# Key gradients transposed by DMA in pairs, in the upper attention layer's backward pass of a four-layer kernel on one Trainium2 core

## The chip, the core and the metric

The kernel runs on one core of one Trainium2 chip. The metric is the time of one execution on the device in microseconds, as the median of several runs. A profile is one further execution, taken with the hardware profiler on. The engines are TensorE (PE for its matmuls, PEld for its weight loads, which run beside matmuls), VectorE (DVE), ScalarE (ACT), GpSimd (POOL) and SyncE (SP), which issues the DMAs; the profile calls the queue of an issuing engine SPq. Data in SBUF lies on 128 partitions; matmul results go to PSUM, which has eight banks.

## The reference

Four residual layers alternate: linear attention (A), gated linear unit (B), A, B, on 2048 tokens of width 512, with weights shared by the two A and by the two B. The kernel returns the output and all gradients for a given output gradient.

```python
def _A_ref(x, wqkv, wo):                      # H = 32 heads of 16
    q, k, v = ...                             # x @ wqkv, split in heads
    phi = lambda t: jnp.where(t > 0, t + 1, jnp.exp(t)) + 1e-6
    pq, pk = phi(q), phi(k)
    kv = jnp.einsum("bhsd,bhse->bhde", pk, v)
    z = jnp.einsum("bhsd->bhd", pk)
    num = jnp.einsum("bhqd,bhde->bhqe", pq, kv)
    den = jnp.einsum("bhqd,bhd->bhq", pq, z)[..., None] + 1e-6
    ...                                       # num / den, heads joined, @ wo
def _B_ref(x, w_gate, w_up, w_down):
    ...                                       # (sigmoid(x @ w_gate) * (x @ w_up)) @ w_down
x = x + _A_ref(_layernorm(x), A_wqkv, A_wo)
x = x + _B_ref(_layernorm(x), B_w_gate, B_w_up, B_w_down)
x = x + _A_ref(_layernorm(x), A_wqkv, A_wo)
x = x + _B_ref(_layernorm(x), B_w_gate, B_w_up, B_w_down)
```

## The kernel before

The tokens are worked on in 16 tiles of 128; two tiles are a pair (`NB2 = 2`). The kernel goes forward through layers 0 to 3, saving what the backward pass needs to DRAM (`sv`), and then backward: `b_bwd_p1` for layer 3, `a_bwd_p1` for layer 2 (the upper attention layer), `b_bwd_p1` for layer 1, `a_bwd_p1` for layer 0, and a tail. The change touches `a_bwd_p1` alone.

Weight gradients are sums over all tokens, so they are made apart, by the object `W` of class `P2`. Its jobs (`b_jobs`, `a_jobs`) each have a "set": one operand of all 16 tiles, up to 1 MB, loaded by one DMA into one of three buffers (`p2_set`, L1363). A job is cut into units, `W.run(n)` runs n of them wherever the code calls it. A unit of the jobs in question is 16 matmuls (L1511); a job has four, its result is evacuated by ScalarE (L1487) in two halves and stored (L1468). When a job's first unit is run, the loads up to two jobs on are called (`prefetch`).

`a_bwd_p1` has two halves. The first makes the query gradients dq and stores them to DRAM. The second (from L1661) is the one of the change. Before its loop, pairs 0 and 1 are loaded (L1702): pk, the key features; dq; hT, the transposed layer input; h, the layer input. A small chain of products follows with units between. Then comes a loop over the 16 tiles (L1772). For tile `st`:

- tiles 0 to 3 transpose dq and pk on TensorE into PSUM (L1785, tile `T2_ps`) and copy them with ScalarE to `pdT`; later tiles find them transposed by the load (L1692, L1674);
- four matmuls give the gradient of the key features (`dpk_ps`, L1791), VectorE multiplies it by the derivative (`dphk`, L1794, and `dk`, L1796, into the pair's tile `dkst`), and on odd tiles the pair is stored (`dqk_store`, L1535);
- on even tiles the next pair's loads are called (`load`, L1802), on odd ones h (L1806);
- VectorE adds the tile before the last to the residual gradient (`add`, L1088 and L1089), and POOL casts it (L292);
- `finish` of the previous tile: twelve matmuls into one bank `dh_ps` (L1756), four each with dqT, pkT and dkT as weights, then the layer norm's backward sums (L1076 on ScalarE, L1081 on VectorE);
- four transposes of this tile's dk on TensorE (L374, `t_ps<-ident,dkstage`) and a copy to `dkT` on ScalarE (L383).

Units are run before the loop, in tile 0 (where there is nothing to finish) and behind the loop; then `W.run(W.left() - HOLD)` (L319) runs all but six of what is left before layer 1 begins. The order of the four computing engines is that of the code. The order of SP's DMAs is not: the framework's scheduler places each DMA in SP's queue when, in its own plan of the run, what it depends on is done and a buffer of its tile's name is free; of those ready, the earlier in the code goes first, and `tc.issue_after` ties one behind another. Tiles of one name in pool `stg` (pk_ld, dq_ld, pkT, hT_ld, h_ld, dkstage) have two buffers.

Of the kernel before, what the change touches and what calls it, by code (L numbers as in the profile page):

```python
# [9 lines left out]
BF16 = mybir.dt.bfloat16  # L10
# [12 lines left out]
P = 128  # L23
NST = S // P
NDC = D // P
# [5 lines left out]
NB = 4  # L31
# [337 lines left out]
def transpose_blocks(k, ps_pool, dst, src_blocks, evac, tag="tp"):  # L369
    nc = k.nc  # L370
    n = len(src_blocks)
    ps = ps_pool.tile([P, 8, P], BF16, name=tag, tag=tag)
    for i, sb in enumerate(src_blocks):
        nc.tensor.transpose(ps[:, i, :], sb, k.ident[:])  # L374
    evac_copy(k, dst, ps[:, 0:n, :], evac)
# [454 lines left out]
def attn_fronts(k, A, pool, small):  # L830
# [38 lines left out]
    def front3(st, bank="ln", evac="scalar"):  # L869
        if st >= NST:  # L870
# [4 lines left out]
                         evac, tag="ln_tp" if bank == "ln" else f"{bank}_ps")  # L875
        f["T"] = pqnT

    def attn_mm(st):
        if st >= NST:
            return  # L880
        pqnT = F_[st]["T"]
        y_ps = F_[st]["y"] = ps_tile(k, "y", [P, D], F32, "y_ps")
# [20 lines left out]
def ab_fwd(k, A, ln, side, nxt=None, out_cb=None, last_cb=None):  # L903
# [3 lines left out]
    with ExitStack() as ctx:  # L907
# [6 lines left out]

        def gu(T, hT, fs, later=False):
            c0, w = FSL[fs]
            ssd_t, hh_t = T["ssd"], T["hh"]
            g_ps = ps_tile(k, "g", [P, 512], F32, "g_ps")
# [15 lines left out]

        def transposes(T, fs):
            hh_t, hhT = T["hh"], T["hhT"]
            fcs = fchunks_of_slice(fs)
# [132 lines left out]
class LnBwd:  # L1070
# [15 lines left out]
    def add(self):  # L1086
        nc = self.k.nc
        nc.vector.scalar_tensor_tensor(self.t[:], self.h, self.ab[:, 1:2], self.t[:], ALU.mult, ALU.add)  # L1088
        nc.vector.scalar_tensor_tensor(self.x[:], self.t[:], self.ab[:, 0:1],  # L1089
                                       self.x[:] if self.res is None else self.res, ALU.add, ALU.add)  # L1090
# [308 lines left out]
class P2:  # L1399
# [7 lines left out]
    def load(self, l, nm, pool=None, part=None):  # L1407
        k, R = self.k, self.R
        src = k.sv[l]["h" if nm == "h" else "gbf"]
        if (l, nm) not in self.ops:  # L1410
            self.ops[l, nm] = (pool or R.big).tile([P, NST, D], BF16, name="p2_a1" if nm == "h" else "p2_a2")
            self.todo[l, nm] = list(range(NST // NB))
        t, todo = self.ops[l, nm], self.todo[l, nm]
        for b in ([part] if part is not None else list(todo)):
            todo.remove(b)
            R.eng().dma_start(out=t[:, b * NB:(b + 1) * NB, :], in_=dram_batch(src, b))
# [115 lines left out]
def dqk_store(k, sv, half, b, src):  # L1532
    n = D // GW
    for g in range(n):
        ins = k.nc.sync.dma_start(out=sv["dqk"][half * n + g, b], in_=src[:, :, g * GW:(g + 1) * GW])  # L1535
    return ins.ins


def a_bwd_p1(k, R, l, W, mk_out_cb=None):
    nc, tc = k.nc, k.tc  # L1540
    sv = k.sv[l]
# [3 lines left out]
    NB2 = 2  # L1545
    with ExitStack() as ctx:
# [9 lines left out]
        with tc.tile_pool(name=f"ab_stg1{l}", bufs=3, side="right", reuse_waits="tile") as stg, \  # L1556
# [60 lines left out]
            for st in range(NST):  # L1617
                with tc.issue_after(k.mt_load):
                    ph_st = phld.get(st)
                T = dict(st=st, ph=ph_st, ph_pair=phld.cur)  # L1620
# [18 lines left out]
                if st >= 1:  # L1639
                    dq_ops(Ts[st - 1])  # L1640
                if st >= DZLAG:
                    accum_dz(Ts[st - DZLAG])
                Ts.append(T)
# [17 lines left out]
        with tc.tile_pool(name=f"ab_stg2{l}", bufs=2, side="right", reuse_waits="tile") as stg, \  # L1661
                tc.tile_pool(name=f"ab_work2{l}", bufs=2, side="right", reuse_waits="tile") as work, \
                tc.tile_pool(name=f"ab_late{l}", bufs=1, reuse_waits="tile") as late:
            pkld = BatchLoader(k, stg, sv["pk"], "pk_ld", nb=NB2)
            hTld = BatchLoader(k, stg, sv["hT"], "hT_ld", nb=NB2)
            hld = BatchLoader(k, stg, sv["h"], "h_ld", nb=NB2)
            out_cb = mk_out_cb(stg) if mk_out_cb is not None else None
            LD, LDH = {}, {}
            pkT = {}
# [7 lines left out]
            def load(p):  # L1677
                if p >= NST // NB2:
                    return
                st0 = p * NB2  # L1680
                pkld.get(st0)
                dq = stg.tile([P, NB2, D], BF16, name="dq_ld")
                if st0 < NB:
                    for g in range(D // GW):
                        nc.sync.dma_start(out=dq[:, :, g * GW:(g + 1) * GW], in_=sv["dqk"][g, p])
                hTld.get(st0)
                if st0 >= NB:
                    dq = dq[:].rearrange("p n d -> p (n d)").rearrange("p (c t) -> p c t", c=NDC)
                    with tc.issue_after(hTld.ins.ins):
                        n = GW // P  # L1690
                        for g in range(D // GW):
                            nc.sync.dma_start(out=dq[:, g * n:(g + 1) * n, :],  # L1692
                                              in_=sv["dqk"][g, p].rearrange("p n w -> (p n) w"), transpose=True)
                        load_pkT(p)
                LD[p] = dict(pk=pkld.cur, dq=dq, hT=hTld.cur)

            def load_h(p):
                if p < NST // NB2:
                    hld.get(p * NB2)
                    LDH[p] = hld.cur  # L1700

            for p in range(2):  # L1702
                load(p)
                load_h(p)
            Nv = late.tile([P, NDC, D], BF16, name="Nv")
            Mv = late.tile([P, NDC, D], BF16, name="Mv")
# [42 lines left out]
            def finish(T):  # L1749
                st = T["st"]  # L1750
                dh_ps = ps_tile(k, "y", [P, D], F32, "dh_ps")
                ops = [(T["dqT"][:, c, :], k.wqkvT[:, c, :]) for c in range(NDC)]
                ops += [(T["pkT"][:, c, :], Mv[:, c, :]) for c in range(NDC)]
                ops += [(T["dkT"][:, c, :], k.wqkvT[:, NDC + c, :]) for c in range(NDC)]
                for i, (lhsT, rhs) in enumerate(ops):
                    nc.tensor.matmul(dh_ps[:], lhsT=lhsT, rhs=rhs, start=(i == 0), stop=(i == len(ops) - 1))  # L1756
                T["ln"] = LnBwd(k, work, small, dh_ps[:], T["h"], k.rstd[l][:, st:st + 1], k.xs[st])
                T["ln"].sums()

            def add(T):  # L1760
                T["ln"].add()
                if out_cb is not None:
                    out_cb(T["st"])
# [3 lines left out]
                nc.scalar.copy(ps[:], dzb[:])  # L1767
                return ps

            prev = prev2 = None  # L1770
            dpk_ps = dpk_begin()
            for st in range(NST):  # L1772
                L = LD[st // NB2]
                e = st % NB2
                pk_st, hT_st = L["pk"][:, e, :], L["hT"][:, e, :]
                T = dict(st=st, h=LDH[st // NB2][:, e, :])
                if e == 0:
                    dkst = stg.tile([P, NB2, D], BF16, name="dkstage")
                own = st < NB
                if own:  # L1780
                    pdT = work.tile([P, 2, NDC, P], BF16, name="pdT")
                    tps = ps_tile(k, "t", [P, 2, NDC, P], BF16, "T2_ps")
                    for a, src in enumerate((L["dq"][:, e, :], pk_st)):
                        for c in range(NDC):
                            nc.tensor.transpose(tps[:, a, c, :], src[:, c * P:(c + 1) * P], k.ident[:])  # L1785
                    nc.scalar.copy(pdT[:], tps[:])
                    T["dqT"], T["pkT"] = pdT[:, 0, :, :], pdT[:, 1, :, :]
                else:
                    T["dqT"], T["pkT"] = L["dq"][:, :, e:NB2 * P:NB2], pkT[st // NB2][:, :, e * P:(e + 1) * P]
                for c in range(NDC):  # L1790
                    nc.tensor.matmul(dpk_ps[:], lhsT=hT_st[:, c * P:(c + 1) * P], rhs=Nv[:, c, :],  # L1791
                                     start=False, stop=(c == NDC - 1), skip_group_check=True)
                dphk = work.tile([P, D], BF16, name="dphk")
                nc.vector.tensor_scalar(dphk[:], pk_st, -EPS, 1.0, ALU.add, ALU.min)  # L1794
                dk = dkst[:, e, :]
                nc.vector.tensor_tensor(dk, dpk_ps[:], dphk[:], ALU.mult)  # L1796
                if e == NB2 - 1:
                    dqk_store(k, sv, 1, st // NB2, dkst[:])
                if st + 1 < NST:
                    dpk_ps = dpk_begin()  # L1800
                if e == 0 and st > 0:
                    load(st // NB2 + 1)  # L1802
                if prev2 is not None:
                    add(prev2)
                    if e == 1:
                        load_h(st // NB2 + 1)  # L1806
                if prev is not None:
                    finish(prev)
                    next(smalls, None)
                else:  # L1810
                    W.run(1)
                dkT = work.tile([P, NDC, P], BF16, name="dkT")
                transpose_blocks(k, k.ps["t"], dkT[:], [dk[:, c * P:(c + 1) * P] for c in range(NDC)], "scalar",
                                 tag="t_ps")
                T["dkT"] = dkT
                prev, prev2 = T, prev
            drain(smalls)
            add(prev2)
            W.run(1)
            finish(prev)  # L1820
            add(prev)


DZLAG = 4
GTLOAD = {4: 2, 6: 3}
SMALL = (("kvbd", P), ("dkvbd", P))
WIDE = ("G", "X")
# [78 lines left out]
```

## Time and profile before

| | us |
|---|---|
| median of 3 runs (1133.23 to 1135.18) | 1133.44 |
| the profiled execution | 1135.02 |
| its span, first to last instruction | 1133.3 |
| TensorE busy in the span | 1109.4 |
| VectorE, ScalarE, POOL busy | 706.9, 484.2, 291.2 |
| loop of the upper layer's second half | 603.1 to 667.2 |
| units alone behind it | 667.2 to about 730 |

The profile is read by lines and tiles of the program: `L1756` is a line of the kernel, `dh_ps<-Mv,pkT` what an instruction writes and reads. A timeline row gives start, duration, engine, line and form; back-to-back matmuls overlap in their durations, so their cost is the distance of their starts. The table by stretches gives busy time of each engine (with the number of instructions), the granted clock of TensorE, the share of the DMA engines and their rate. A DMA has two times: that of its issue on SP, and its landing, when its semaphore is complete.

### The profile page before, as it was taken

To read this page: it belongs to the slowest core of one execution; us is meant where nothing else is said; L and a number is where in the kernel's file an instruction comes from. 1 tells how busy PE (TensorE), PEld (TensorE's weight loads), DVE (VectorE), ACT (ScalarE), POOL (GpSimd) and SP (SyncE) were. 2 spreads that over 40 slices of the span, in tenths; PEclk is the share of its full clock that TensorE was granted. 3 is DMA by queue.
4 is the path that set the end of the run, shared out by engine and by line. 5 is a ranking of instruction groups with operands and counts; after the bars stand their busy time and mean duration, and the time that the engine had idled before them with its cause. 6 is when DMAs were issued, how large, how long until landed. Compare 5 with 4: busy or idle time off the path is not lost.

```text
span 1133.3 us, 20011 instructions
## 1 busy us (share of the span) xinstructions
PE 1109.4 (98%) x7468; PEld 648.8 (57%) x7468; DVE 706.9 (62%) x1344; ACT 484.2 (43%) x909; POOL 291.2 (26%) x518
## 2 busy tenths in 40 slices
PE   8979999998999999999999999999999999999998
PEld 4444554444555555554456468855546745448888
DVE  6788886778776456664975850166664976852211
ACT  6676666555756543433625431224324515410000
POOL 5647776435666400000110220000000110210000
PEclk9999999999999999999999999999999999999999
DMA  8967999855899999997899997799998899969996
GB/s 270 309 197 212 273 282 283 245 142 183 223 294 265 269 261 262 302 255 207 222 244 313 220 260 237 195 283 289 257 283 260 205 282 289 241 194 298 263 205 192
DMA packets 413682, 282.36 MB, mean 249 GB/s; under 512 B 198608, under 2 KB 399504, under 8 KB 409744
## 3 DMA queue, kind: packets, MB, share of 16 engines
q1 hardware_dynamic: 412432, 280.03, 90.3%
q8 instruction: 58, 0.95, 0.3%
q10 hardware_dynamic: 1152, 1.05, 0.3%
q14 instruction: 40, 0.33, 0.1%
HBM read 125.44 MB, written 115.70 MB: 213 GB/s over the span
## 4 chain that ended last, share of the span: by engine, by line
PE 89%; DVE 6%; DMA 3%; ACT 1%; issue 1%; POOL 0%; DVEq 0%; SPq 0%; POOLq 0%
PE p_ps L1511 18%; PE dh_ps L1252 13%; PE dh_ps L1756 7%; PE p_ps L1495 7%; PE y_ps L956 6%; PE dhh_ps L1110 6%; PE g_ps L922 6%; PE u_ps L922 6%; PE T_ps L1209 3%; PE dpk_ps L1791 2%; PE GT_ps L1652 2%; PE dp_ps L1624 2%; PE y_ps L884 2%; PE t_mm L616 2%; PE X_ps L624 2%; PE t_ps L374 1%
## 5 line engine op out<-in xcount | busy, mean ns | idle before, releaser
L1511 PE MATMUL p_ps<-p_set,p_a 128*128 128x256 bf16 (+1 forms) x2032 | 210.1, 264 | 0.0
L1511 PEld LDWEIGHTS <-p_a 128*128 128x128 bf16 x2048 | 185.9, 98 | 22.2
L1132 DVE TENSOR_TENSOR dd<-dhh_ps,ssd 128x512 bf16<-128x512 f32 x144 | 82.4, 629 | 121.3 <-PE dhh_ps L1110 117.4
L930 POOL TENSOR_TENSOR ssd_t<-hh_t,oms 128x512 bf16<-128x512 bf16 (+1 forms) x96 | 100.7, 1060 | 50.1 <-ACT out_t L226 13.5
L1252 PEld LDWEIGHTS <-ddT 128*128 128x128 bf16 (+1 forms) x704 | 67.6, 98 | 74.6 <-DMA ddT<-dd 2.4
L922 PEld LDWEIGHTS <-hT 128*128 128x128 bf16 x768 | 72.5, 98 | 65.2 <-DVE hT L381 1.4
L1084 POOL TENSOR_SCALAR ab<-c 128x2 f32<-128x2 f32 x64 | 12.4, 194 | 377.9 <-DVE junk L1081 364.7
L1211 ACT COPY ddT<-T_ps 128x1024 bf16<-128x1024 bf16 (+1 forms) x72 | 58.8, 819 | 115.2 <-PE T_ps L1209 62.0
L1076 ACT ACTIVATE t_sb<-dh_ps,rstd_all 128x512 f32<-128x512 f32 x64 | 44.0, 688 | 115.7 <-issue 65.0
L922 PE MATMUL g_ps<-wg,hT 128*128 128x512 bf16 (+1 forms) x384 | 90.0, 357 | 0.4 <-DVE hT L381 0.4
L924 ACT ACTIVATE ssd_t<-g_ps 128x512 bf16<-128x512 f32 (+1 forms) x96 | 53.4, 556 | 86.1 <-PE g_ps L922 80.3
L922 PE MATMUL u_ps<-wu,hT 128*128 128x512 bf16 (+1 forms) x384 | 90.0, 357 | 0.0
L1485 DVE TENSOR_TENSOR dw_stg<-p_ps,dw_stg 128x512 bf16<-128x512 f32 (+3 forms) x43 | 28.1, 653 | 98.1 <-PE p_ps L1511 81.4
L929 DVE TENSOR_TENSOR hh_t<-u_ps,ssd_t 128x512 bf16<-128x512 f32 (+1 forms) x96 | 60.4, 631 | 44.0 <-PE u_ps L922 34.2
L1252 PE MATMUL dh_ps<-wgT,ddT 128*128 128x512 bf16 (+1 forms) x352 | 85.2, 379 | 0.0
L1252 PE MATMUL dh_ps<-wuT,ddT 128*128 128x512 bf16 (+1 forms) x352 | 81.3, 379 | 0.8 <-DMA ddT<-dd 0.7
L956 PE MATMUL y_ps<-wd,hhT 128*128 128x512 bf16 (+1 forms) x352 | 81.3, 379 | 0.6 <-DVE x L958 0.6
L1495 PE MATMUL p_ps<-p_a,p_set 128*128 128x512 bf16 (+1 forms) x352 | 81.2, 379 | 0.0
L1110 PE MATMUL dhh_ps<-wdT,gTb 128*128 128x512 bf16 x336 | 74.2, 357 | 0.0
L956 PEld LDWEIGHTS <-hhT 128*128 128x128 bf16 (+1 forms) x352 | 34.2, 98 | 41.1 <-issue 0.7
L1081 DVE SCALAR_TENSOR_TENSOR junk<-t_sb,h_ld 128x512 bf16<-128x512 f32 x48 | 37.2, 774 | 28.9 <-ACT t_sb L1076 23.7
L926 ACT ACTIVATE oms<-g_ps 128x512 bf16<-128x512 f32 (+1 forms) x96 | 52.8, 550 | 3.9 <-POOL ssd_t L930 3.7
(227 smaller groups left out, 1824.2 us busy)
## 6 DMA issues: line engine op xcount, KB each, us to landing
p_set<-sv_hdd SPq DMA_DIRECT2D x30, 1024.0 KB, 6.2
sv_ssd<-ssd_t SPq DMA_DIRECT2D x32, 688.0 KB, 4.2
ssd<-sv_ssd SPq DMA_DIRECT2D x24, 688.0 KB, 5.1
sv_hdd<-dd SPq DMA_DIRECT2D x24, 512.0 KB, 5.0
sv_hdd<-hh_t SPq DMA_DIRECT2D x32, 320.0 KB, 4.4
p_a<-sv_h SPq DMA_DIRECT2D x16, 512.0 KB, 6.5
p_set<-sv_dqk SPq DMA_DIRECT2D x8, 1024.0 KB, 7.5
h_ld<-sv_h SPq DMA_DIRECT2D x24, 256.0 KB, 4.7
```

Source lines behind the costliest of these rows:

```text
L922: nc.tensor.matmul(ps[:, 0:w], lhsT=hT[:, kc, :], rhs=w_sb[:, kc, c0:c0 + w], start=(kc == 0), stop=(kc == NDC - 1))
L924: nc.scalar.activation(ssd_t[:, 0, c0:c0 + w], g_ps[:, 0:w], ACT.Sigmoid)
L929: nc.vector.tensor_tensor(hh_t[:, c0:c0 + w], u_ps[:, 0:w], ssd_t[:, 0, c0:c0 + w], ALU.mult)
L930: nc.gpsimd.tensor_tensor(ssd_t[:, 1, c0:c0 + w], hh_t[:, c0:c0 + w], oms[:, 0:w], ALU.mult)
L956: nc.tensor.matmul(y_ps[:], lhsT=T["hhT"][0:r, fc, :], rhs=k.wd[0:r, fc, :], start=(fc == 0), stop=(fc == NFC - 1))
L1110: k.nc.tensor.matmul(ps[:, 0:w], lhsT=gT[:, jc, :], rhs=k.wdT[:, jc, c0:c0 + w], start=(jc == 0), stop=(jc == NDC - 1))
L1132: k.nc.vector.tensor_tensor(dd_part(dd, a, fs), ps[:, 0:w], ssd[:, a, c0:c0 + w], ALU.mult)
L1211: nc.scalar.copy(out[:, :, 0:nfull, :], tps[:, :, 0:nfull, :])
L1252: nc.tensor.matmul(T["dh"][:], lhsT=T["ddT"][0:r, dd_block(a, fc), :], rhs=(k.wuT, k.wgT)[a][0:r, fc, :], start=(i == 0), stop=(i == 2 * N ...
L1495: nc.tensor.matmul(ps[0:r, :], lhsT=set_t[:, st, c * P:c * P + r], rhs=self.ops[j["l"], "g"][:, st, :], start=(st == 0), stop=(st == NST - 1))
L1511: nc.tensor.matmul(ps[:, icl * w:(icl + 1) * w], lhsT=self.ops[j["l"], "h"][:, st, ic * P:(ic + 1) * P], rhs=set_t[:, st, 0:w], start=(st ...
L1756: nc.tensor.matmul(dh_ps[:], lhsT=lhsT, rhs=rhs, start=(i == 0), stop=(i == len(ops) - 1))
```

## The change

In layer 2, dk of pairs 2 to 6 (tiles 4 to 13) is no longer transposed by TensorE. At the end of the pair's odd tile, one DMA transposes both tiles' dk from SBUF to SBUF (`dkTs`). Since dkT is there later, `finish` of such a tile comes two tiles behind instead of one, so `todo` holds the tiles that wait for `finish` and `done` those that wait for `add`. From tile 4 on a unit is run in each tile. `load` is split: `load` takes pk and hT, `load_T` dq and pkT; in layer 2 `load_T` is called on odd tiles behind `finish`, and h is loaded on even tiles. In layer 0 (`DK_DMA[0] = ()`) the steps of the loop stay as they were; there, as in layer 2, `dq` of the first pairs is loaded behind hT.

```diff
@@ loads
                 pkld.get(st0)
+                hTld.get(st0)
+                LD[p] = dict(pk=pkld.cur, hT=hTld.cur)
+
+            def load_T(p):
+                if p >= NST // NB2:
+                    return
+                st0 = p * NB2
                 dq = stg.tile([P, NB2, D], BF16, name="dq_ld")
                 if st0 < NB:
                     for g in range(D // GW):
                         nc.sync.dma_start(out=dq[:, :, g * GW:(g + 1) * GW], in_=sv["dqk"][g, p])
-                hTld.get(st0)
-                if st0 >= NB:
+                else:
...
-                LD[p] = dict(pk=pkld.cur, dq=dq, hT=hTld.cur)
+                LD[p]["dq"] = dq
...
             for p in range(2):
                 load(p)
+                load_T(p)
                 load_h(p)
@@ the loop
-            prev = prev2 = None
+            by_dma = DK_DMA[l]
+            todo, done = [], []
...
                 if e == NB2 - 1:
-                    dqk_store(k, sv, 1, st // NB2, dkst[:])
+                    if p in by_dma:
+                        dkTs = stg.tile([P, NB2 * NDC, P], BF16, name="dkTs")
+                        nc.sync.dma_start(out=dkTs[:], in_=dkst[:].rearrange("p n d -> p (n d)"), transpose=True)
+                        for i, Ti in enumerate((todo[-1], T)):
+                            Ti["dkT"] = dkTs[:, i * NDC:(i + 1) * NDC, :]
+                    dqk_store(k, sv, 1, p, dkst[:])
                 if st + 1 < NST:
                     dpk_ps = dpk_begin()
                 if e == 0 and st > 0:
-                    load(st // NB2 + 1)
-                if prev2 is not None:
-                    add(prev2)
-                    if e == 1:
-                        load_h(st // NB2 + 1)
-                if prev is not None:
-                    finish(prev)
+                    load(p + 1)
+                    if not by_dma:
+                        load_T(p + 1)
+                if done:
+                    add(done.pop(0))
+                if by_dma:
+                    if e == 0 and p >= 2:
+                        load_h(p)
+                elif e == 1 and st > 1:
+                    load_h(p + 1)
+                if todo and st - todo[0]["st"] > (todo[0]["st"] // NB2 in by_dma):
+                    finish(todo[0])
+                    done.append(todo.pop(0))
                     next(smalls, None)
                 else:
                     W.run(1)
-                dkT = work.tile([P, NDC, P], BF16, name="dkT")
-                transpose_blocks(k, k.ps["t"], dkT[:], [dk[:, c * P:(c + 1) * P] for c in range(NDC)], "scalar",
-                                 tag="t_ps")
-                T["dkT"] = dkT
-                prev, prev2 = T, prev
+                if by_dma:
+                    if e == 1:
+                        load_T(p + 1)
+                    if p >= by_dma[0]:
+                        W.run(1)
+                if p not in by_dma:
+                    T["dkT"] = work.tile([P, NDC, P], BF16, name="dkT")
+                    transpose_blocks(k, k.ps["t"], T["dkT"][:], [dk[:, c * P:(c + 1) * P] for c in range(NDC)],
+                                     "scalar", tag="t_ps")
+                todo.append(T)
             drain(smalls)
-            add(prev2)
-            W.run(1)
-            finish(prev)
-            add(prev)
+            for T in done:
+                add(T)
+            for T in todo:
+                W.run(1)
+                finish(T)
+                add(T)
...
+DK_DMA = {2: range(2, NST // 2 - 1), 0: ()}
```

More of the change, by code (lines that the diff above doesn't have):

```diff
@@ L1756, in finish @@
                     nc.tensor.matmul(dh_ps[:], lhsT=lhsT, rhs=rhs, start=(i == 0), stop=(i == len(ops) - 1))
+                T["h"] = LDH[st // NB2][:, st % NB2, :]
                 T["ln"] = LnBwd(k, work, small, dh_ps[:], T["h"], k.rstd[l][:, st:st + 1], k.xs[st])
@@ L1768, in dpk_begin @@
                 return ps
-            prev = prev2 = None
+            by_dma = DK_DMA[l]
+            todo, done = [], []
             dpk_ps = dpk_begin()
             for st in range(NST):
-                L = LD[st // NB2]
-                e = st % NB2
+                p, e = divmod(st, NB2)
+                L = LD[p]
                 pk_st, hT_st = L["pk"][:, e, :], L["hT"][:, e, :]
-                T = dict(st=st, h=LDH[st // NB2][:, e, :])
+                T = dict(st=st)
                 if e == 0:
                     dkst = stg.tile([P, NB2, D], BF16, name="dkstage")
-                own = st < NB
-                if own:
+                if st < NB:
                     pdT = work.tile([P, 2, NDC, P], BF16, name="pdT")
@@ L1788, in a_bwd_p1 @@
                 else:
-                    T["dqT"], T["pkT"] = L["dq"][:, :, e:NB2 * P:NB2], pkT[st // NB2][:, :, e * P:(e + 1) * P]
+                    T["dqT"], T["pkT"] = L["dq"][:, :, e:NB2 * P:NB2], pkT[p][:, :, e * P:(e + 1) * P]
                 for c in range(NDC):
```

## The prediction

> **What bounds the kernel now.** I read the page first, for the engine that sets the end.
>
> ```profile
> PE 1109.4 (98%) x7468; PEld 648.8 (57%) x7468; DVE 706.9 (62%) x1344; ACT 484.2 (43%) x909; POOL 291.2 (26%) x518
> ...
> PE 89%; DVE 6%; DMA 3%; ACT 1%; issue 1%; POOL 0%; DVEq 0%; SPq 0%; POOLq 0%
> ```
>
> TensorE is busy for 98% of the span and holds 89% of the chain that ended last. So a microsecond of TensorE work taken away is a microsecond gained, and one of TensorE waiting is one lost, wherever it falls. Next the table by stretches: the tile loop runs from 603.1 to 667.2 us, then weight gradients alone until about 730.
>
> ```profile
> core 0: us, PE busy (x) PEld busy (x) DVE busy (x) ACT busy (x) POOL busy (x), PEclk, DMA share, GB/s
> ...
> 633.00:648.00 15.00, 15.00 (x84) 7.33 (x83) 12.44 (x25) 6.98 (x16) 3.25 (x8) 1.00 0.87 228
> ...
> 682.00:697.00 15.00, 15.00 (x140) 13.44 (x138) 0.00 (x0) 2.34 (x4) 0.00 (x0) 1.00 0.77 259
> ```
>
> TensorE has no free time in either stretch (15.00 of 15.00) at full granted clock. VectorE is near its limit in the first (12.44) and idle in the second. Then TensorE's timeline for one tile:
>
> ```profile
> 622.19 0.39 PE L374 MATMUL t_ps<-ident,dkstage 128*128 128x128 bf16 x4
> 622.42 1.03 PE L1791 MATMUL dpk_ps<-Nv,hT_ld 128*128 128x512 bf16 x4
> 623.28 1.03 PE L1756 MATMUL dh_ps<-wqkvT,dq_ld 128*128 128x512 bf16 x4
> 624.14 1.03 PE L1756 MATMUL dh_ps<-Mv,pkT 128*128 128x512 bf16 x4
> 625.01 1.03 PE L1756 MATMUL dh_ps<-wqkvT,dkT 128*128 128x512 bf16 x4
> ```
>
> Instructions overlap, so cost is read from start to start: four transposes take 0.23 (622.19 to 622.42), each group of four wide matmuls 0.86, a tile 3.68. Last, the order in which SP issues DMAs at the head of the loop:
>
> ```profile
> 600.43 1.21 SPq L1685 DMA_DIRECT2D dq_ld<-sv_dqk  x2
> 601.68 0.60 SPq L1147 DMA_DIRECT2D hT_ld<-sv_hT  x1
> ...
> 604.12 0.37 SPq L1363 DMA_DIRECT2D p_set<-sv_hdd  x1
> 604.59 0.38 SPq L1833 DMA_DIRECT2D sv_G<-woT_GT  x1
> 605.89 0.33 SPq L1363 DMA_DIRECT2D p_set<-sv_hdd  x1
> ...
> 608.15 1.29 SPq L1535 DMA_DIRECT2D sv_dqk<-dkstage  x2
> 609.54 0.66 SPq L1147 DMA_DIRECT2D pk_ld<-sv_pk  x1
> ```
>
> Two things are to be seen. SP does not follow the code's order: the set of 605.89 belongs to a job whose load the code calls at 662.86; it went as soon as a buffer came free. And transfers land in the order of issue: the two sets (1 MB each) land at 610.2 and 614.8, G between them at 611.7, and pk of 609.54 only at 617.1.
>
> **What goes.** Tiles 4 to 13 lose four transposes each: 40 at 0.0555 (0.222 a tile, from 625.87 to 626.09) is 2.22 us off TensorE. Their ten ScalarE copies (576 ns, dkT's row) were under matmuls and give nothing. [...]
>
> **What moves.** Twelve weight-gradient units go into tiles 4 to 15, one more in tile 5 (nothing to finish there) and one more at the end. A unit is 16 matmuls, 1.75 us; 14 leave the run after the loop, so the sum is nil. A tile of the middle becomes 0.87 + 2.59 + 1.75 = 5.21. VectorE's 3.1 a tile gets room; a unit's evacuation (587 ns on ScalarE every second unit) has ScalarE's 8 free us of 15 to hide in, and POOL's casts follow VectorE's adds as before. The transposed loads of the next pair move a tile later: for pair 4 its buffers are free in tile 7 after the finish of tile 5, its reader is tile 10's finish some 13 us on, and dq's row has 2.7 to 7.1 to landing: hidden, and beyond 13 us TensorE would wait for the rest. The weight loads after the loop start some 22 us later; their readers come about 40 us after that, and they land in 7.
>
> **What is added, 1: dk by DMA.** Nearest row, the same shape SBUF to SBUF in another stage:
>
> ```profile
> L1216 SPq DMA_TRANSPOSE ddT<-dd x17: 1237/1277/3868, 499.4 to 847.1; - x17
> ...
> DMA to landing us min/median/max: 3.2/4.4/7.5
> ```
>
> Count from the start of the odd tile: dpk ends at 0.87, VectorE's product (691 ns, L1796) about 1.75, issue at 2.0. The first reader, the even tile's finish in the next tile, needs it at 5.21 + 0.87 + 8 x 0.216 = 7.8. With the median it lands at 6.4: hidden. In tile 5, shorter at 4.37, the reader comes at 7.0: still hidden. But in tiles 7 and 11 a weight job has just ended and its buffer is free, so SP issues the next 1 MB set at the tile's start. The rows of sets give 5.5 to 6.6 us to landing where little stands ahead; then the finished gradient's store (0.95 between landings), hT (0.7) and the transpose (0.85): 8.2 to 9.3, late by 0.4 to 1.5. If the store or hT falls behind, nothing is late. I take 0.75 for each of two pairs, 1.5 in all; ends 0 and, with the row's 7.5 at all five pairs (1.7 each), 8.5. Queued behind a waiting finish on TensorE is everything: unit, dpk, and through them the rest. SP's own work per pair goes from about 7.1 of 7.35 us to about 8.8 of 10.42.
>
> **What is added, 2: a load too many.** Before the loop, pairs 0 and 1 get their dq. In the loop `load_T(p + 1)` stands under `e == 1` with no lower bound, so tile 1 loads pair 1's dq again (two DMAs, 256 KB), and tile 2's transposes read that second copy. They are due at 610.27 in the old time, with no slack. The two buffers of dq hold pair 0, read until 606.4, and the first copy of pair 1, which nothing reads. If the reload gets the buffer that is free first, it is issued behind the first copy's landing (about 606) and ahead of the set of 605.89: it lands behind G, at 612.1 and 612.6, and TensorE waits 1.5 to 2.0. If it must wait for pair 0's buffer it stands behind that set: 615.2 and 615.6, a wait of about 5; in pk's place (the same condition of release, issued 609.54) it lands near 617 and costs 6.6. Nothing gives this back, because TensorE has no other wait in the loop. I take the first, 1.8, by the row of the eager set, with 0 and 6.6 as ends.
>
> **What is added, 3: order at the head.** In both layers dq is now queued behind hT for pairs 0 and 1. Tile 0 begins with dq's transposes, which already wait 0.6 (601.90, 602.33); they would end near 603.4, dpk starting 0.4 later. In the lower layer dq has landed before it is needed: 0. Bounds 0 and 0.4; I take 0.4. The later load of h is needed by VectorE's sums of a finish two tiles on; TensorE would feel it only through the one dh bank, which it needs 5.2 us later.
>
> **Sum.** -2.22 + 0.4 + 1.8 + 1.5 = +1.5. The profiled execution took 1135.02 (span 1133.3 and 1.7 around it), 1.6 above the median of 1133.44; I put the difference on the median: 1134.9.
>
> **Rivals.** Late reload (slower): the second copy waits for pair 0's buffer and lands behind both sets. For it: pk's load of pair 2 has that very condition and went at 609.54. Against it: the unread buffer is free sooner. -2.2 + 0.4 + 5.2 + 1.5 = +4.9, 1138.3; it decides as soon as the reload is issued behind the set of 605.89. Such a wait leaves TensorE idle for over 4 us, which no stretch of this trace behind its start shows (longest 1.7, clock 1.00 throughout). [...]
>
> All covered: reload and sets are early enough, the waits are 0 and the 2.2 stays: 1131.2 to 1132.5, taken as 1131.6. For it: DMA latencies of 3.2 to 4.4 are common. Against: the two queues of 1 MB loads are in the trace.
>
> Late at every pair: SP puts the next pair's transposed loads of dq (1.25 us of SP each, their buffer free at 1.74 in tile 7 and on) ahead of dk's, and all five pairs wait: -2.2 + 0.4 + 1.8 + 8.5 = +8.5, 1141.9. Against: SP has 1.6 us a pair to spare.
>
> **Chances.** Forecast 0.40, late reload 0.27, covered 0.25, late at every pair 0.08. A measurement of this kernel tells about 0.2% (2.3 us) from no change. Faster by more needs the whole 2.2 and a little: a quarter of covered, 0.06. Within: the rest of covered and three quarters of the forecast, 0.49. Slower: 0.45. The range 1131.1 to 1140.0 leaves out the last rival and a sliver on either side. The forecast's own is 1133.4 to 1136.5.
>
> **What would show it.** Transposes of dkstage 128 to 88, tiles 6 to 13 at 5.21 start to start: the saving. A wait of TensorE's weight load for dq in tile 2, between a wide matmul's end and T2: the reload, with ten dq issues of 128 KB in place of eight, and their place beside the 1 MB sets. Waits for dkTs in tiles 8 and 12: the sets; in all of 6, 8, 10, 12, 14: the last rival. No wait for dq in tile 2, or dk landing before 7.8 behind a set, would make the sum wrong.

## The result and the profile after

The changed kernel takes 1142.47 us (median of 9 runs, 1139.33 to 1146.76), the kernel before in the same comparison 1135.15 (9 runs, 1133.23 to 1139.23). The ratio is 1.007, with a 95% interval of 1.0057 to 1.0082. It is slower, and by more than the range allowed.

The profiled execution of the changed kernel took 1139.33 us, span 1137.6. That is the fastest of its runs, so its trace shows only part of the loss. A second profile of it (label a0 below) has a span of 1144.0. First the row of engines on the page:

```profile
PE 1112.5 (98%) x7428; PEld 649.8 (57%) x7428; DVE 706.1 (62%) x1344; ACT 478.7 (42%) x899; POOL 288.6 (25%) x518
```

TensorE runs 40 matmuls fewer (7428 for 7468) and is busy 3.1 us longer. A shorter list of work is busy for longer because of the clock: this trace has three stretches of 3.41 us at half the granted clock (at 65.05, 256.20 and 665.80 us), some 1.7 us each, and the profile of before has none in its span. The first two lie in the forward layers, which the change does not touch, and a second profile of before (b0 below) has two there as well. The third is looked at below. The table by stretches, for the two stretches shown before:

```profile
core 0: us, PE busy (x) PEld busy (x) DVE busy (x) ACT busy (x) POOL busy (x), PEclk, DMA share, GB/s
633.00:648.00 15.00, 12.59 (x75) 7.08 (x74) 7.98 (x15) 3.36 (x8) 1.62 (x4) 1.00 1.04 228
682.00:697.00 15.00, 15.00 (x109) 10.32 (x108) 7.10 (x14) 3.98 (x9) 2.43 (x6) 1.00 0.79 255
```

VectorE got its room (12.44 to 7.98 in the first), and TensorE, which had no free time there, now idles 2.41 us, all in one wait. The share of the DMA engines went from 0.87 to 1.04; over the whole loop it lay between 0.87 and 1.10 before, too. TensorE's timeline of a tile without a wait:

```profile
644.94 1.03 PE L1799 MATMUL dpk_ps<-Nv,hT_ld 128*128 128x512 bf16 x4
645.80 1.03 PE L1763 MATMUL dh_ps<-wqkvT,dq_ld 128*128 128x512 bf16 x4
646.66 1.03 PE L1763 MATMUL dh_ps<-Mv,pkT 128*128 128x512 bf16 x4
647.53 1.03 PE L1763 MATMUL dh_ps<-wqkvT,dkTs 128*128 128x512 bf16 x4
648.39 1.91 PE L1511 MATMUL p_ps<-p_set,p_a 128*128 128x256 bf16 x16
650.14 1.03 PE L1799 MATMUL dpk_ps<-Nv,hT_ld 128*128 128x512 bf16 x4
```

From 644.94 to 650.14 are 5.20, as forecast: the transposes are gone and the unit costs 1.75. Now TensorE's waits from 603 to 700, and its timeline in tile 12:

```profile
engine line waited for: us in total, times, longest us
PE dh_ps L1763 <- DMA dkTs<-dkstage: 4.9, 3, 2.4
```

```profile
661.40 1.03 PE L1763 MATMUL dh_ps<-wqkvT,dq_ld 128*128 128x512 bf16 x4
662.26 1.03 PE L1763 MATMUL dh_ps<-Mv,pkT 128*128 128x512 bf16 x4
665.57 1.70 PE L1763 MATMUL dh_ps<-wqkvT,dkTs 128*128 128x512 bf16 x4 [2.28 <-DMA dkTs<-dkstage]
667.06 2.97 PE L1511 MATMUL p_ps<-p_set,p_a 128*128 128x256 bf16 x16
669.86 1.03 PE L1799 MATMUL dpk_ps<-Nv,hT_ld 128*128 128x512 bf16 x4
```

From start to start, 662.26 to 665.57 are 3.31 where 0.86 is needed: 2.45 lost. The same in tile 8 (638.88 to 642.32) is 2.58. Behind the second wait the four matmuls take 1.49 and the unit 2.80 instead of 0.86 and 1.75: another 1.68, at half the clock. SP's queue ahead of that wait:

```profile
655.58 0.37 SPq L1147 DMA_DIRECT2D pk_ld<-sv_pk  x1
656.05 0.49 SPq L1363 DMA_DIRECT2D p_set<-sv_hdd  x1
656.63 0.38 SPq L1468 DMA_DIRECT2D dwp_wu<-dw_stg  x1
657.12 3.31 SPq L1808 DMA_TRANSPOSE dkTs<-dkstage  x1
```

The set lands at 663.67, the store at 664.65, dkTs at 665.52: in the order of issue, dkTs 8.40 after its own. In tile 7 the same order gives 640.46, 641.38 and 642.27 (8.53). The reload of pair 1's dq stands where the prediction's likeliest case put it, ahead of the second set (603.62 here, 605.89 before):

```profile
602.14 1.39 SPq L1692 DMA_DIRECT2D dq_ld<-sv_dqk  x2
603.62 0.66 SPq L1363 DMA_DIRECT2D p_set<-sv_hdd  x1
```

It landed at 608.04 and 608.43 and cost 0.41. To find what else there is, I cut the traces into stages at first matmuls. The "loop" here goes from the first dpk of layer 2 to layer 1's first `dhh`, so it holds the same units in every kernel; "layer 1" goes from there to its last `dh_ps`.

| us | before | before again (b0) | after | after again (a0) |
|---|---|---|---|---|
| loop with all units | 128.19 | 128.18 | 133.44 | 132.84 |
| layer 1 | 132.30 | 132.89 | 133.89 | 136.74 |
| all other stages | 872.8 | 873.1 | 870.3 | 874.4 |
| span | 1133.31 | 1134.17 | 1137.61 | 1143.97 |

So there are two losses, one in the loop (4.7 to 5.3), and one in layer 1, a stage that the diff does not touch (1.0 to 4.4). The other stages differ by 4 us between the two profiles of one and the same kernel (870.3 and 874.4), so below I compare these two.

### The profile page after: what moved, and what is told of

Same layout as the page of the kernel before. It is cut to its first block, busy times and chain, and to the rows that moved or that the text cites. A ratio compares the mean times of both kernels' runs of the same rounds, so it can differ in the third digit from the quotient of the medians.

```text
span 1137.6 us, 19908 instructions
## 1 busy us (share of the span) xinstructions
PE 1112.5 (98%) x7428; PEld 649.8 (57%) x7428; DVE 706.1 (62%) x1344; ACT 478.7 (42%) x899; POOL 288.6 (25%) x518
## 3 DMA queue, kind: packets, MB, share of 16 engines
q10 hardware_dynamic: 1152, 1.05, 0.3%
## 5 line engine op out<-in xcount | busy, mean ns | idle before, releaser
L1511 PE MATMUL p_ps<-p_set,p_a 128*128 128x256 bf16 (+1 forms) x2032 | 213.3, 265 | 0.0
```

The costliest lines, as they stand in the source:

```text
L1511: nc.tensor.matmul(ps[:, icl * w:(icl + 1) * w], lhsT=self.ops[j["l"], "h"][:, st, ic * P:(ic + 1) * P], rhs=set_t[:, st, 0:w], start=(st ...
```

## Experiments

The ratio of each is against the kernel before on the same chip. Theory: the loop's loss is dk's transpose landing behind a set. First rivals: the reload, and the units themselves. Waits in this section are the idle times that the profile gives (2.41 and 2.28, where the distances of starts gave 2.58 and 2.45 lost).

**The set tied behind dkTs in odd tiles.**

```diff
-                        nc.sync.dma_start(out=dkTs[:], ..., transpose=True)
+                        dk_ins = nc.sync.dma_start(out=dkTs[:], ..., transpose=True)
...
-                        W.run(1)
+                        with ExitStack() as order:
+                            if e == 1 and p in by_dma:
+                                order.enter_context(tc.issue_after(dk_ins.ins))
+                            W.run(1)
```

> The change, with one tie added: in an odd tile whose pair goes by DMA, the set load that the tile's unit calls is queued on SP behind the transposing DMA. Theory 1 (the 1 MB set loads of tiles 7 and 11 stand ahead of dk's transposes, 2.4 and 2.3 us of TensorE waiting, and the second wait halves the clock for 3.4 us): TensorE waits for dkTs under 0.3 us in all, no half clock behind it, time 1 to 2.2 us under before, ratio 0.998 to 0.9995. Rival A (a transposing DMA is too slow for this distance, whatever stands ahead): waits of over 1 us stay in tiles 8 and 12, ratio 1.003 or more. Rival B (the units moved into the loop cost by their traffic, wherever it stands): the waits go to other loads, ratio 1.003 or more.

Measured: 1144.44, ratio 1.007 [1.0053, 1.0087]; loop 135.50. The wait in tile 8 is gone (dkTs of pair 3 lands 4.52 after issue), but one of 2.84 stands in tile 10. SP's queue there:

```profile
644.41 2.55 SPq L1698 DMA_TRANSPOSE dq_ld<-sv_dqk  x2
647.08 1.23 SPq L1674 DMA_TRANSPOSE pkT<-sv_pk  x1
648.36 0.58 SPq L1363 DMA_DIRECT2D p_set<-sv_hdd  x1
...
652.06 3.22 SPq L1808 DMA_TRANSPOSE dkTs<-dkstage  x1
```

The tied set comes behind the transposing loads that hold SP, at 648.36, and then stands ahead of the next dkTs, which lands 8.43 after issue. The order of a pair was mended and the next pair paid, so the forecast of no wait failed. The reload stood in the same place as before, behind the first set and G, but the set took 9.12 to land (602.50 to 611.62, in the first profile 6.65), and the wait for the reload was 3.83.

**No reload:** `if e == 1:` ahead of `load_T(p + 1)` becomes `if e == 1 and st > 1:`.

> The change without the second load of pair 1's dq (load_T only from tile 3 on). Theory 1: the reload landed in time but for 0.1 us, so 0 to 0.5 us under the changed kernel, ratio to before 1.005 to 1.008. Rival C (the reload pushes back what follows and so makes the later waits): 3 us or more under the changed kernel, ratio under 1.004.

Measured: 1143.52, ratio 1.0062 [1.004, 1.0084]; loop 133.70. No wait for dq is left, those for dkTs are 0.31, 2.55 and 2.70. The reload is a part that changes from run to run (0.41 in the first profile, a wait of 3.83 above), but the waits for dkTs are there without it.

**The units in tiles 4 to 15 alone**, dk by TensorE, one tile behind.

```diff
-DK_DMA = {2: range(2, NST // 2 - 1), 0: ()}
+DK_DMA = {2: (), 0: ()}
...
+                if in_loop and p >= 2:      # in_loop: layer 2
+                    W.run(1)
```

> The units alone: one unit in each of tiles 4 to 15 of the upper layer, dk transposed by TensorE as before, finish one tile behind, loads called where they were. Theory 1: no transposing DMA is late, TensorE waits nowhere in the loop, time that of before within 1 us, ratio 0.999 to 1.001. Rival B: the sets that now share the loop with its loads cost 3 us or more, ratio 1.003 or more, with waits for hT, dq or pk in the loop.

Measured: 1135.97, ratio 1.0001 [0.9989, 1.0013]; loop 128.18, layer 1 132.13. The units with their sets cost nothing by themselves, although the share of the DMA engines is 1.05 from 633 to 648 here as well.

**Sets early**, two units in tile 0, so that jobs end one tile earlier: `W.run(1)` in the branch without a finish becomes `W.run(2 if by_dma and st == 0 else 1)`.

> The change with two units in tile 0 instead of one, so that jobs end one unit earlier and the sets are issued at the start of even tiles (6, 10, 14), a tile ahead of the next transposing DMA; no tie. Theory 1: the sets have landed when dk's transposes are issued; waits for dkTs under 0.5 us in all, ratio 0.998 to 1.0. Rival A: waits in tiles 8 and 12 as in the change, ratio 1.004 or more. Rival B: ratio 1.003 or more.

Measured: 1142.82, ratio 1.0058 [1.0045, 1.0071]; loop 134.50. The set meant for the start of tile 10 was not issued there:

```profile
651.00 1.25 SPq L1808 DMA_TRANSPOSE dkTs<-dkstage  x1
652.31 1.75 SPq L1535 DMA_DIRECT2D sv_dqk<-dkstage  x2
654.16 2.88 SPq L1698 DMA_TRANSPOSE dq_ld<-sv_dqk  x2
657.14 1.25 SPq L1674 DMA_TRANSPOSE pkT<-sv_pk  x1
658.48 0.53 SPq L1363 DMA_DIRECT2D p_set<-sv_hdd  x1
...
663.34 3.59 SPq L1808 DMA_TRANSPOSE dkTs<-dkstage  x1
```

SP is busy without a break from 651.0 to 658.4, and the set slips until only five DMAs stand between it and the next dkTs; the wait there is 3.43. The reload, again behind a set that took 9.12, cost a wait of 1.95. The mechanism (a set ahead in the queue) was seen again, but as long as SP has a backlog, shifting the set only chooses the pair that pays.

**The changed kernel again**, as a control.

> The changed kernel unaltered, for a second profile. If the waits are set by the order of SP's queue, the waits of TensorE for dkTs in tiles 8 and 12 come again within 0.5 us (2.41 and 2.28 before), the wait for the reload in tile 2 stays near 0.1, and layer 1 (bwd1's first dhh to its last dh_ps) again takes 133.9 (132.3 in the kernel before). If they are set by chance in the DMA queues, one of them moves by more than 1 us, and the half clock comes behind another wait or not at all. Median ratio 1.005 to 1.008.

Measured: 1144.51, ratio 1.0066 [1.0049, 1.0083]. The wait in tile 12 is 2.88, that in tile 8 only 0.78: the order in SP's queue was the same, but the set landed 6.21 after its issue instead of 7.84, and dkTs 6.90 after its own. So a set ahead costs about 0.8 to 2.9, and not 2.4 each time as expected: the order is fixed, the size goes by how fast the set lands. Layer 1 came to 136.74.

**No units in the loop**: the two lines that run a unit from tile 4 on are left out, so no set falls into the tiles with DMA transposes.

> The changed kernel without the units of weight gradients in tiles 4 to 15 (they run behind the loop, so their sets are loaded there). dk by DMA, two tiles behind, stays. A tile is then 3.46, and dkTs is needed 3.46 + 0.87 + 1.73 = 6.1 us after the odd tile's start, issued at about 2.0: 4.1 us for a transpose that without a set took 3.1 to 5.5. Theory of sets ahead in the queue: waits of 0 to 1.4 per pair, 0 to 3 over five pairs, the loop with its units 126 to 130. Rival, the transposing DMAs themselves are too much for SP (8.8 us of SP per pair against 6.9): all five pairs wait 1.9 or more, 9 in all, and the loop with its units takes 135 or more, ratio 1.006 or more.

Measured: 1148.66, ratio 1.011 [1.009, 1.013]; loop 138.00. Waits for dkTs of 1.86, 0.37, 2.98, 0.07 and 2.00, though dkTs now lands only 3.2 to 4.3 after issue. It is issued late: in tile 9, which starts at 638.14, at 643.83, where I reckoned 2.0 behind the start.

```profile
636.55 2.56 SPq L1698 DMA_TRANSPOSE dq_ld<-sv_dqk  x2
639.21 1.25 SPq L1674 DMA_TRANSPOSE pkT<-sv_pk  x1
640.57 0.51 SPq L1147 DMA_DIRECT2D h_ld<-sv_h  x1
...
642.51 1.22 SPq L1698 DMA_TRANSPOSE dq_ld<-sv_dqk  x1
643.83 1.24 SPq L1808 DMA_TRANSPOSE dkTs<-dkstage  x1
```

Here the rival is the nearer, though three pairs wait long and not all five: without the units a pair should last 6.92 us, and SP takes 9.6 from one dkTs to the next (643.83, 653.43, 663.08), nearly without a break. The units are what makes room for the transposes, and what puts sets ahead of them.

**Pairs 2, 4 and 6 alone by DMA**, and no reload: `DK_DMA = {2: (2, 4, 6), 0: ()}`.

> Two edits of the changed kernel: only pairs 2, 4 and 6 (tiles 4, 5, 8, 9, 12, 13) have their dk transposed by DMA, pairs 3 and 5, ahead of whose transposes a set was loaded, by TensorE; and pair 1's dq isn't loaded a second time. Units and sets stay. Theory of too little lead: the sets of tiles 7 and 11 have landed (663.7 at the latest in the changed kernel) before the next transpose of dk, so no wait over 0.3 us in the loop; 24 transposes less are 1.3 us: the loop with its units comes to 126.9 to 127.5, ratio 0.999 to 1.002. Rival, a full queue: a set slips to just ahead of another transpose, as in the two shifted versions, and one wait of 2 to 3.5 us comes in tile 10 or 14: 129 to 131, ratio 1.002 to 1.005.

Measured: 1136.77, ratio 1.0003 [0.9992, 1.0015]; loop 129.14. One wait, of 1.91 for pair 2, with no set ahead: four loads (dq, pkT, pk, hT) stood ahead, and dkTs landed 6.77 after issue. So a set is one way to be late, not the only one. The loop's time lies in the rival's range, but without the rival's cause.

**Three tiles behind**, and no reload.

```diff
-                if todo and st - todo[0]["st"] > (todo[0]["st"] // NB2 in by_dma):
+                if todo and st - todo[0]["st"] > 2 * (todo[0]["st"] // NB2 in by_dma):
```

> Two edits of the changed kernel: input gradients of tiles 4 to 13 come three tiles behind instead of two, and pair 1's dq isn't loaded a second time. Theory of too little lead (dk's transpose lands in the order of issue behind a 1 MB set, 8.4 to 8.5 us after issue, and is needed 5.8 us after issue): the reader is now 5.2 us later, so every wait for dkTs in the loop is 0 and no half clock follows; the loop with its units loses 2.41 + 2.28 + 1.7 of its 133.4 and comes to 127 (the kernel before: 128.2). Time 0.999 to 1.002 of before, by whether layer 1 keeps its extra 1.6. Rival, a full queue (the transposing DMAs hold SP, and what does not wait for dkTs waits for the transposed dq or pk of the next pair, whose buffers now come free a tile later): waits of 2 us and more for dq_ld or pkT in tiles 10 to 15, and the loop at 131 to 134; ratio 1.003 to 1.007.

Measured: 1135.27, ratio 0.9995 [0.9985, 1.0005]; loop 126.97 against 128.19 before. There is no wait for dkTs and no half clock in the loop, and the set still stands ahead in tile 7, with dkTs landing 7.77 after its issue:

```profile
633.95 0.50 SPq L1363 DMA_DIRECT2D p_set<-sv_hdd  x1
634.54 0.41 SPq L1468 DMA_DIRECT2D dwp_wg<-dw_stg  x1
635.49 2.60 SPq L1808 DMA_TRANSPOSE dkTs<-dkstage  x1
```

It lands at 643.26 and is read at 646.70. With two tiles behind it would have been read one tile (5.2 us) earlier, at 641.50, and so 1.8 too early. For pair 3 this shows the cause: the queue is as full as before and only the reader is later. For pair 5 the run is no such test, because the set went earlier here (651.91, landed at 657.79, before dkTs was issued at 659.35). The version without the reload differs by the lag alone, and its loop took 133.70. What eats the gain is layer 1, with 135.35.

**Layer 1.** In the traces, queue q8 (kind "instruction") moves 16 KB 58 times in 7468 matmuls, one for 128.8 on average, so it seems to go by TensorE's progress through its program. With 40 matmuls gone, it comes 6.4 us later in layer 1 (89.7 behind the stage's start, 83.4 before). DMA view of 8 us around it, changed kernel, then the kernel before at the same place of the stage; a digit or a rate is 0.2 us:

```profile
DMA  4999889889963629999000004999999999999999
GB/s 193 385 413 385 330 358 413 332 315 374 345 236 102 154 55 207 206 179 28 0 3 9 9 10 92 289 276 269 241 219 211 163 250 324 317 305 294 284 289 302
...
q8 instruction: 1, 0.02, 1.1%
```

```profile
DMA  9997868989963499999779999999999999999999
GB/s 390 413 330 248 303 275 341 428 322 343 323 236 113 101 221 215 210 215 182 152 163 221 215 202 211 169 214 313 302 294 292 287 276 307 269 297 294 264 245 157
```

Two transposing DMAs (ddT, around 210 GB/s) run here in both. In the changed kernel the 16 KB fall among them, and the DMA engines move next to nothing (0 to 10 GB/s) for 1.0 us; the second ddT holds SP 2.19 instead of 1.27, and what follows on SP is some 1.1 late, until TensorE waits for ddT. Whether the meeting is the cause can be tried without touching the loop, with the 48 warm-up matmuls at the program's start, whose result is not used.

**The kernel before again**, as a control.

> The kernel before unaltered, for a second profile. The open part of the loss: layer 1 (first dhh to last L1252 matmul) took 132.3 in the kernel before and 133.7 to 136.7 in all versions with 24 or 40 fewer matmuls ahead of it. If that is tied to the program, this run gives 132.0 to 132.6, with the 16 KB transfer of queue q8 again 83.3 us behind the stage's start; if it is chance, it can come out anywhere from 132 to 136.

Measured: 1135.94, ratio 0.9997 [0.9983, 1.0012]; transfer at 83.4, layer 1 132.89 (0.3 above what I had allowed).

**The kernel before with 40 warm-up matmuls fewer:** `range(WARM)` becomes `range(WARM - 40)`.

> The kernel before with 40 of the 48 warm-up matmuls at its start left out (they compute nothing that is used), and nothing else changed: dk by TensorE, old order. In the traces queue q8 moves 16 KB once for about every 128 matmuls, so it follows TensorE's count of instructions; 40 matmuls fewer move it by 6.4 us, from 83.3 to 89.7 behind the start of layer 1's stage, where in the changed kernel it meets two transposing DMAs and all queues move some 25 GB/s for 1 us. Theory of the moved code transfer: layer 1's stage takes 133.5 to 136 here too, ratio 1.001 to 1.003, though dk's transposes are untouched. Rival, something that dk's DMA transposes leave behind: layer 1 stays at 132.0 to 132.6, ratio 0.999 to 1.001.

Measured: 1137.22, ratio 1.0007 [0.9996, 1.0019]; transfer at 89.6, layer 1 135.46, with waits for ddT of 2.05 and 1.83. The same place of the stage:

```profile
DMA  8999878989983789990000059999999999999999
GB/s 275 330 303 303 275 330 358 418 336 393 358 307 113 157 182 215 186 35 0 3 8 10 9 106 288 276 266 227 214 216 147 253 328 323 312 294 282 289 300 266
...
q8 instruction: 1, 0.02, 1.1%
```

The old code has the new code's gap. The whole time does not settle it: the ratio lies in the rival's range, and all other stages of this run took 871.0, where the two profiles of before have 872.8 and 873.1. The stage does.

**The changed kernel, and the version three tiles behind, with 40 more:**

```diff
-            for i in range(WARM):
-                nc.tensor.matmul(warm_ps[:], lhsT=k.ident[:], rhs=k.ident[:], start=True, stop=True)
+            for i in range(WARM + 40):
+                n = P if i < 16 else 16
+                nc.tensor.matmul(warm_ps[:, 0:n], lhsT=k.ident[:], rhs=k.ident[:, 0:n], start=True, stop=True)
```

> The changed kernel with 40 more warm-up matmuls at its start (88 in place of 48, most of 16 columns, about the same time). Theory of the moved code transfer: the count of matmuls ahead of layer 1 is that of the kernel before again, the transfer falls 83.3 us behind the stage's start, and the stage takes 132.0 to 132.8 instead of 133.9 and 136.7; the waits for dkTs in tiles 8 and 12 stay (2 to 3 us, one of them at least). Ratio 1.003 to 1.006. Rival: layer 1 stays at 133.5 or more.

Measured: 1140.92, ratio 1.0041 [1.0022, 1.0059]; transfer at 83.3, layer 1 132.66; the waits for dkTs stay, up to 3.16.

> The version three tiles behind and without the second load of pair 1's dq, with 40 more warm-up matmuls at its start. Theory of the moved code transfer: the loop with its units stays at 127.0 (before 128.2) and layer 1 falls from 135.35 to 132.0 to 132.8: 1.0 to 1.4 us better than before, ratio 0.997 to 0.9995. Rival: layer 1 stays at 134 or more and the ratio at 0.9995 to 1.001.

Measured: 1135.30, ratio 0.9986 [0.9973, 0.9999]; loop 125.95, transfer at 83.4, layer 1 132.98. This is the one version whose interval lies below the kernel before, by about 0.1% and only just. TensorE's waits from 740 to 880 in it:

```profile
PE dh_ps L1253 <- DMA ddT<-dd: 1.5, 2, 1.0
```

All fourteen traces together: in the five with the transfer at 83.3 to 83.4 (both of before, units alone, and the two with 40 more) layer 1 takes 132.1 to 133.0; in the nine with it at 89.3 to 90.4 it takes 133.7 to 136.7. The place of the loss fits: in all nine TensorE waits for ddT (0.4 to 2.1) at 103.6 to 105.4 behind the stage's start, 14 to 16 behind the transfer; of the five, only the last version waits there (0.5).

Two parts of the loss are something else. a0 and the versions three tiles behind and with pairs 2, 4 and 6 had lost 0.7 to 1.1 before this transfer came. And in a0 and in the version with sets early, a wait for ddT of 1.99 and 2.06 near the stage's end was followed by a stretch of half clock (at 859.90 and 859.64), some 1.7 more. That the count of matmuls ahead makes the loss is shown by the warm-up matmuls. That it does so by the transfer at 89.7 is argued from the place, since the transfers before and behind it moved as well.

## Why the prediction was wrong

**Removal, right.** -2.22 forecast. In the version with all else cured the loop is 125.95 against 128.18: -2.23.

**Units free, right.** 128.18 with the units alone, 5.20 a tile.

**Head, 0.4: not there.** The stretch from the first `GT_ps` matmul to the loop is 24.72 in the changed kernel and in the second profile of before; the 25.67 of the first profile held a wait that does not always come. In the lower layer I wrote 0; the new order of loads waits for dq there between 0 and 1.1 by the run.

**Reload, 1.8: the place was right, the size too high in this profile** (0.41; 1.0 in a0, 1.2 in the changed kernel with 40 more). It landed behind G, as reckoned (607.34, then 608.04 and 608.43), but set and G went out 4.9 earlier than before (599.25 and 599.70, before 604.12 and 604.59) while TensorE reached tile 2 only 2.2 earlier (608.1, before 610.3). With the set tied and with sets early its place was the same, behind the first set and G and ahead of the second, but the first set took 9.12 to land, and the waits were 3.83 and 1.95. So the mechanism is the one forecast in all these versions, never the rival's, and the size goes by the set, 0.4 to some 4.

**The failed step: "I take 0.75 for each of two pairs".** The two pairs, the cause and the order were right, and so was the need (7.8 behind the tile's start, measured 7.78) and the issue (2.0, measured 1.8). What failed is the set's time to landing, for which I took rows "where little stands ahead" (5.5 to 6.6), though my own reading of the loop's head has a set that took 8.9 (605.89 to 614.8). In the loop the sets took 7.84 and 7.62 and were issued 0.7 behind the tile's start; hT, counted with 0.7, did not stand between. So dkTs landed at 10.3 and 10.2 instead of 8.2 to 9.3. Measured 2.58 and 2.45 instead of 0.75 each; with 0.35 for pair 2, which I had as hidden, 5.38 instead of 1.5. Where a set took 6.21 (tile 7 of a0), the wait was 0.78, about what I forecast. Why a set takes longer is not shown. The DMA engines' load is the likely reason: their share was 1.04 and 1.08 in the two stretches here, and in a0 0.78 around the quick set and 1.06 around the slow one (8.06).

**Left out of the sum: the half clock.** It cost 1.68 behind a wait of 2.45. The loop adds up: 125.95 + 0.41 + 5.38 + 1.68 = 133.42, measured 133.44.

**Not seen at all: layer 1**, +1.6 in this profile, +3.9 in the second pair of profiles, some 1.7 of it half clock. The sum has no term for any stage behind the loop, and I did not ask what 40 instructions fewer shift.

Forecast +1.5; the terms measured are -2.23 + 0.41 + 5.38 + 1.68 + 1.59 = +6.8, beside +7.3 between the medians. That these two agree is in part luck: the profile from which the terms are read is only 4.3 longer than that of before, because its other stages came out 2.5 shorter. The forecast time also stood on 1133.44, where the comparison has 1135.15 for the kernel before. The rival "late at every pair" (1141.9) comes nearest in number, but not in mechanism: two pairs waited long, behind sets, and not all five behind the next pair's loads.

## What to carry to other kernels

Price a new DMA by the landing time behind what SP's queue really holds in that stretch, with the DMA share of that stretch beside it, and where it must be late, move its reader rather than its place in the queue. Here two nearly full queues (SP's issue and the DMA engines) handed a delay on to the next transfer: with the set tied, the wait left tile 8 and one of 2.84 came in tile 10; with sets early, SP was busy without a break from 651.0 to 658.4, and TensorE waited 3.43 for the next dkTs. All of this was worth 0.1% at most, since the transposes that it replaces took only 2.2 us of TensorE. When a stage that was not touched gets slower, compare what falls together with what in it: here 40 matmuls fewer moved a 16 KB transfer of queue q8 in layer 1 by 6.4 us, and as many unused matmuls at the start, left out or added, tested that.

## What the runs showed of the hardware

**The granted clock falls to half for 3.41 us at a time.** In the changed kernel's trace such stretches start at 65.05, 256.20 and 665.80, and one at 1136.84 is cut short by the end. Their distances are whole multiples of 3.413 us (191.15 is 56 of them, 600.75 is 176, 1071.79 is 314). Where the whole trace is divided into stretches of that length at these places, TensorE idled 2.50, 2.60, 2.28 and 2.24 us in the four ahead of those at half clock; no other stretch had more than 1.99, and the clock behind it stayed at 1.00. In the profile of before none had more than 1.76 up to the end of TensorE's work, and the clock stayed at 1.00 as well (the ends of matmuls are modelled). The two waits of the changed kernel's loop, each with the stretch that follows:

```profile
core 0: us, PE busy (x) PEld busy (x) DVE busy (x) ACT busy (x) POOL busy (x), PEclk, DMA share, GB/s
638.50:641.90 3.40, 1.41 (x7) 0.44 (x5) 1.82 (x3) 0.00 (x0) 0.62 (x1) 1.00 1.38 117
641.90:645.30 3.40, 2.98 (x22) 2.16 (x23) 0.91 (x3) 0.94 (x3) 0.19 (x1) 1.00 0.96 211
662.40:665.80 3.40, 1.12 (x7) 0.31 (x5) 1.30 (x2) 0.00 (x0) 0.62 (x1) 1.00 1.23 231
665.80:669.20 3.40, 3.40 (x15) 1.95 (x14) 0.91 (x3) 0.78 (x2) 0.19 (x1) 0.50 0.79 178
```

The first wait is spread over two stretches (1.99 and 0.42) and costs no clock; the second lies in one (2.28) and costs 1.68. So what these waits cost went by where they fell as well as by their length: waits of 2.70 (without the reload) and 2.84 (with the set tied) cost nothing more.

**A 16 KB transfer of queue q8 among two transposing DMAs.** The queue (kind "instruction") moves 16 KB 58 times in the changed kernel's 7428 matmuls. In layer 1 one of these transfers came at 823.92, between the issue of two transposing DMAs at 822.94 and 824.28. TensorE did not wait then (busy for 2.00 of 2.00 us from 824.21 to 826.21), but the DMA engines moved 0 to 10 GB/s for 1.0 us, as they did in the kernel before with 40 warm-up matmuls fewer, and the stage lost 1 to 4, of which half clock and earlier waits are a part in some runs. Why the transfers stop, and how a gap of 1 us becomes waits of up to 2.1 some 15 us on, stays open.

**A transposing DMA holds SP.** In the changed kernel the issue of dkTs takes 1.23 to 1.27 us for the three pairs without a set just ahead, and 4.02 and 3.31 for the two behind one (tiles 7 and 11). What SP has to issue next waits with it: the store of dk came at 637.81, 0.05 behind the end of the 4.02.
